# A GEGLU feed-forward kernel: x loaded in halves of the model dimension, first weights in 128 KB pieces over both queues

## The chip, the core and the metric

The kernel runs on one core of a Trainium2 chip. A core has a matrix engine (TensorE, "PE" in the profile; its weight loads are "PEld"), a vector engine (VectorE, "DVE"), a scalar engine (ScalarE, "ACT"), GpSimd ("POOL") and SyncE ("SP"). SBUF is the on-chip memory with 128 partitions, PSUM holds the matrix engine's sums in eight banks. Data come from device memory by DMA; here SP and ACT issue DMAs on a hardware queue each (q1 and q10 in the profile) and POOL issues them on a software queue (q0). An engine works through its program in order, and a DMA that it issues is one step of that program. The metric is the device time in microseconds (us).

## The reference

```python
B, S, D, F = 32, 32, 1024, 3584
x: (B, S, D), w_gate, w_up: (D, F), w_down: (F, D)      # bf16
def reference(x, w_gate, w_up, w_down):
    return (gelu(x @ w_gate) * (x @ w_up)) @ w_down     # gelu by the tanh formula
```

So there are N = 1024 tokens, a model dimension of 1024 and a hidden dimension of 3584.

## The kernel before

The kernel has two stages, and each engine has a program written out by hand (`prog_sp`, `prog_act`, `prog_pool`, `prog_pe`, `prog_dve`); semaphores tie them together.

Stage 1 computes hT, the hidden activations with the hidden dimension on partitions, in 28 chunks of 128 hidden units. A chunk needs a gate product G and an up product U. Each is a sum over eight slices of the model dimension (dk 0 to 7) of a 128x128 piece of weights times xT, the transposed x. Row 8p+dk of the weights stands on partition p in slice dk, so that a partition reads one contiguous row for each slice. ACT applies the GELU to G (L383, result in one of four buffers `tb`), DVE multiplies it by U out of PSUM and writes hT (L409). Stage 2 computes out = hT.T @ w_down in 17 jobs of 28 matmuls (L367), which ACT and DVE evict and SP stores.

The work of stage 1 is cut into "parts". Parts 0 to 7 are chunks 0 to 7 for tokens 0 to 255, one PSUM bank each (G in one half of the bank, U in the other). Parts 8 to 15 are the same chunks and banks for tokens 256 to 511, so part 8 can't start before part 0's product has left bank 0, and so on. From part 16 on a part has 512 tokens and two banks. The list `steps` sets PE's order: `together(range(0, 8), 6)` runs slices 0 to 5 over all eight parts side by side (8 G matmuls, 8 U matmuls for each slice), then slices 6 and 7 part after part; `together(range(8, 12), 5)` does the same with four parts and five slices; all others run one after the other.

x comes in three pieces of tokens, XA (0 to 255), XB (256 to 511) and XC2 (512 to 1023). It is put untransposed into `xs`, a part of hT that is written late, and DVE transposes it into xT in 32x32 blocks, one instruction for each piece and slice (L402): T0 to T7 of XA, then B0 to B7 of XB, then C0 to C7 of XC2. The order of DVE's work is written out in `dve_order`: the products E0 to E15 of parts 0 to 15 stand between the transposes.

The weights of chunks 0 to 7 (`wgbig` and `wubig`) are loaded by `early_loads`, which SP runs as side 0 and ACT as side 1. ACT runs it at the head of its program, before its first GELU. On each side there are 16 DMAs, in this order: two of XA (128 KB each, 512 bytes a packet), four of the weights of slices 0 and 1 (128 KB, 1 KB a packet), six of slices 2 to 7 (256 KB, 2 KB a packet; SP loads `wg`, ACT `wu`), two of XB (128 KB, 512 bytes a packet), two of XC2 (256 KB, 512 bytes a packet). The later chunks' weights come in DMAs of 1 MB by `load_w`, `wg` on SP and `wu` on POOL, once PE has finished with the buffer; the first of them wait for XC2 (`gate_w`).

Before its first real matmul PE runs NDUMMY = 9 matmuls of 512 columns on constants (L324), and waits for the last of them.

Of the kernel before, what the change touches and what calls it, by code (L numbers as in the profile page):

```python
# [5 lines left out]
P = 128  # L6
# [78 lines left out]
def bass_standalone__geglu_ffn__sampling_kernel(  # L85
# [7 lines left out]
    xf = x.flatten_outer_dims()  # L93
# [5 lines left out]
    DK = D // P  # L99
# [21 lines left out]

    XC = N // 32
    XE = D // 4
    XA, XB, XC2 = (0, 256), (256, 512), (512, 1024)
    XPIECES = [XA, XB, XC2]
    W0 = [(0, 0, 512), (0, 512, 1024), (1, 0, 512), (1, 512, 1024)]
    W0 += [(k, 0, 1024) for k in range(2, DK)]

    parts = []
    for t0, t1 in (XA, XB):
        for m in range(NBIG):
            parts.append((m, t0, t1, (m, 0, 256), (m, 256, 512)))
    NSHORT = len(parts)
# [4 lines left out]
    NPART = len(parts)  # L142
# [10 lines left out]

    steps = []

    def together(ps_, ks):
        for dk in range(ks):
            for key in ("G", "U"):
                for p in ps_:
                    steps.append((p, key, dk))  # L160
        for p in ps_:
            for key in ("G", "U"):
                for dk in range(ks, DK):
                    steps.append((p, key, dk))

    together(range(0, 8), 6)
    together(range(8, 12), 5)
    for p in range(12, NPART):
        together([p], 0)


    dve_order = [("T", dk) + XA for dk in range(DK)]
    mix = "E0 E1 B0 E2 B1 E3 B2 E4 B3 E5 B4 E6 B5 E7 B6 B7 C0 E8 C1 E9 C2 E10 E11 C3 C4 E12 C5 E13 C6 E14 C7 E15"
    for w in mix.split():
        if w[0] == "E":
            dve_order.append(("E", int(w[1:])))
        else:
            dve_order.append(("T", int(w[1:])) + (XB if w[0] == "B" else XC2))
    dve_order += [("E", p) for p in range(NSHORT, NPART)]

    jobs = []
# [9 lines left out]
        return ji % 2 == 0  # L191

    out_r = of.rearrange("(tc p) d -> p tc d", p=P)
    x_r = xf.rearrange("(c i) (a e) -> a i c e", i=32, a=4)
    wg_r = w_gate.rearrange("(p k) f -> p k f", k=DK)
    wu_r = w_up.rearrange("(p k) f -> p k f", k=DK)
    wd_r = w_down.rearrange("(m p) d -> p m d", p=P)

    C_PE = _Clock("pe")
    C_ACT = _Clock("act")  # L200
    C_DVE = _Clock("dve")
    C_POOL = _Clock("pool")
    Q_X = {(q, s): _Clock(f"x{i}{s}", 16) for i, q in enumerate(XPIECES) for s in range(2)}
    Q_W0 = {(w, p): _Clock(f"{w}0k{p[0]}c{p[1]}", 16) for p in W0 for w in ("wg", "wu")}
    Q_WG = [_Clock(f"wg{j}", 16) for j in range(NG)]
    Q_WU = [_Clock(f"wu{j}", 16) for j in range(NG)]
    Q_WD_SP = _Clock("wd_sp", 16)
# [5 lines left out]
    ctx = _Ctx()  # L213

    with ExitStack() as es:
# [24 lines left out]
        def wbuf(w, buf):  # L240
            if buf == "s":
                return small[w]
            o = 0 if buf == "lo" else GSZ * P
            return big[w][:, :, o:o + GSZ * P]
# [9 lines left out]
        def load_w(ew, eng, w, j):  # L254
            c0, gsz, buf = groups[j]
            q = (Q_WG if w == "wg" else Q_WU)[j]
            ctx.set((w, j), ew.do(lambda: eng.dma_start(  # L257
                wbuf(w, buf)[:, :, 0:gsz * P], w_r[w][:, :, c0 * P:(c0 + gsz) * P]), clock=q))

        def load_x(ew, eng, q, side):  # L260
            c0, c1 = q[0] // 32, q[1] // 32
            for a in (2 * side, 2 * side + 1):
                v = ew.do(lambda: eng.dma_start(
                    xs[32 * a:32 * (a + 1), c0:c1, :], x_r[a, :, c0:c1, :]), clock=Q_X[(q, side)])
            ctx.set(("x", q, side), v)

        def load_w0(ew, eng, w, p):
            k, f0, f1 = p
            ctx.set((w + "0", p), ew.do(lambda: eng.dma_start(
                big[w][:, k, f0:f1], w_r[w][:, k, f0:f1]), clock=Q_W0[(w, p)]))  # L270

        def early_loads(ew, eng, side):
            load_x(ew, eng, XA, side)
            for k in range(2):
                for w in ("wg", "wu"):
                    load_w0(ew, eng, w, W0[2 * k + side])
            for k in range(2, DK):
                load_w0(ew, eng, ("wg", "wu")[side], W0[2 + k])
            load_x(ew, eng, XB, side)
            load_x(ew, eng, XC2, side)  # L280

        def gate_w(ew, j):
            if war[j] is None:
                for s in range(2):
                    ew.wait(Q_X[(XC2, s)], ctx.get(("x", XC2, s)))
                return -1
            ew.wait(C_PE, ctx.get(("U", last_part[war[j]])))
            return war[j]
# [26 lines left out]
                    osb[:, tc, col0:col0 + ncols]), clock=Q_OUT)  # L315
            sp.wait(Q_OUT, last)

        NDUMMY = 9

        def prog_pe(eng):  # L320
            pe = _Eng(ctx, eng, C_PE)
            v = None
            for i in range(NDUMMY):
                v = pe.do(lambda: eng.matmul(ps[:, 7, :], ones_w, ones_x,  # L324
                                             start=True, stop=True), mark=(i == NDUMMY - 1))
            pe.wait(C_PE, v)
            opened = set()
            for (i, key, dk) in steps:
                m, t0, t1, gs, us = parts[i]
                w, (bank, f0, f1) = ("wg", gs) if key == "G" else ("wu", us)  # L330
                buf, slot, j = slot_of[m]
                if j is None:
                    p = next(p for p in W0 if p[0] == dk and p[1] <= m * P < p[2])
                    pe.wait(Q_W0[(w, p)], ctx.get((w + "0", p)))
                else:
                    pe.wait((Q_WG if w == "wg" else Q_WU)[j], ctx.get((w, j)))
                if bank in bank_before[i]:
                    pe.wait(C_DVE, ctx.get(("D", bank_before[i][bank])))
                for q in XPIECES:
                    if q[0] < t1 and t0 < q[1]:  # L340
                        pe.wait(C_DVE, ctx.get(("T", dk, q)))
                first = (i, bank) not in opened
                opened.add((i, bank))
                last = (dk == DK - 1)
                v = pe.do(lambda: eng.matmul(  # L345
                    ps[:, bank, f0:f1],
                    wbuf(w, buf)[:, dk, slot * P:(slot + 1) * P],
                    xT[:, dk, t0:t1],
                    start=first, stop=last and (key == "U" or gs[0] != us[0]),
                ), mark=last)  # L350
                if last:
                    ctx.set((key, i), v)
            pe.wait(Q_WD_SP, ctx.get("wd_sp_total"))
            pe.wait(Q_WD_POOL, ctx.get("wd_pool_total"))
            bank_last_job = {}
            for ji, (tc, col0, ncols, b) in enumerate(jobs):
                if b in bank_last_job:
                    pj = bank_last_job[b]
                    pe.wait(C_ACT if evac_eng_is_act(pj) else C_DVE, ctx.get(("E", pj)))
                else:  # L360
                    pe.wait(C_DVE, ctx.get(("D", owner[b])))
                bank_last_job[b] = ji
                v = None
                for m in range(FM):
                    pe.wait(C_DVE, ctx.get(("D", last_part[m])))
                    last = (m == FM - 1)
                    v = pe.do(lambda: eng.matmul(  # L367
                        ps[:, b, 0:ncols],
                        hT[:, m, tc * P:(tc + 1) * P],
                        wd[:, m, col0:col0 + ncols],  # L370
                        start=(m == 0), stop=(m == FM - 1),
                    ), mark=last)
                ctx.set(("O", ji), v)
# [18 lines left out]
        def prog_dve(eng):  # L392
            dve = _Eng(ctx, eng, C_DVE)

            for what in dve_order:
                if what[0] == "T":
                    dk, q = what[1], what[2:]
                    for s in range(2):
                        dve.wait(Q_X[(q, s)], ctx.get(("x", q, s)))
                    src = xs[:, q[0] // 32:q[1] // 32, :].rearrange(  # L400
                        "p c (j k) -> p c j k", k=DK)[:, :, :, dk]
                    ctx.set(("T", dk, q), dve.do(lambda: eng.transpose(  # L402
                        xT[:, dk, q[0]:q[1]].rearrange("p (c i) -> p c i", i=32), src)))
                else:
                    i = what[1]
                    m, t0, t1, _gs, (ub, u0, u1) = parts[i]
                    dve.wait(C_ACT, ctx.get(("A", i)))
                    dve.wait(C_PE, ctx.get(("U", i)))
                    ctx.set(("D", i), dve.do(lambda: eng.tensor_tensor(  # L409
                        hT[:, m, t0:t1], t_bufs[i % NTB][:, 0:t1 - t0], ps[:, ub, u0:u1], ALU.mult)))  # L410
# [56 lines left out]
```

## Time and profile before

| what | number |
|---|---|
| median of 3 runs | 301.82 us (301.38 to 302.17) |
| the profiled execution | 300.94 us, of which the span from first to last instruction is 299.6 us |
| first real matmul of PE | 5.60 us |
| idle of PE between 5.60 and 35.1 us | at 16.5, 19.7, 20.5 and 25.5 us, the longest 0.6 us |
| first GELU of ACT | 16.86 us |
| DVE waits for a DMA of x | until 4.83 us, and 1.06 us until 19.19 us |
| start of part 16 on PE | 35.12 us |
| start of stage 2 on PE | 200.83 us |

The span begins with the first instruction of the program; the 1.3 us between span and device time lie outside the instructions. In a timeline row stand the start, the length, the engine, the line, the operation, what it writes and reads, and the number of merged instructions; "SPq" and "ACTq" are the engine's sequencer, here issuing a DMA. In a row of the windows, busy time and number of instructions of each engine are followed by the granted TensorE clock, the mean busy share of the 16 DMA engines and what they moved in GB/s.

### The profile page before, as it was taken

How to read it: one execution, taken by the hardware profiler on the slowest of the kernel's cores; microseconds unless marked ns; L12 is line 12 of the kernel's file. 1: busy time of each engine (PE TensorE's matmuls, PEld its weight loads, DVE VectorE, ACT ScalarE, POOL GpSimd, SP SyncE). 2: the span in 40 equal slices, each digit the busy share in tenths (PEclk: the TensorE clock that was granted, in tenths of full speed). 3: DMA queues.
4: the chain of work that ended last, by engine and by line, in shares of the span. 5: the costliest groups of instructions: out<-in, count | busy, mean ns of one | idle time of the engine just before them, and what ended most of it. 6: DMA issues, size and time to landing. Idle time of an engine off the chain costs nothing.

```text
span 299.6 us, 3392 instructions
## 1 busy us (share of the span) xinstructions
PE 294.0 (98%) x1485; PEld 147.6 (49%) x1509; DVE 60.2 (20%) x96; ACT 41.4 (14%) x75; POOL 7.0 (2%) x12
## 2 busy tenths in 40 slices
PE   7999999999999999999999999999999999999997
PEld 3878744444444444444444444444444444444456
DVE  3259811211111211111211112210000000000000
ACT  1042211111211111211111211110000000000000
POOL 0001001020001002000000000000000000000000
DMA  8998002947007400952103000000000100010001
GB/s 239 381 223 270 13 1 81 343 142 278 2 0 251 171 0 7 357 198 63 77 0 142 0 0 2 0 0 18 20 18 18 35 20 18 18 36 19 18 18 37
DMA packets 19118, 26.43 MB, mean 88 GB/s; under 512 B 1056, under 2 KB 13472, under 8 KB 19104
## 3 DMA queue, kind: packets, MB, share of 16 engines
q1 hardware_dynamic: 13344, 14.68, 15.0%
q0 software_dynamic: 2176, 8.39, 7.9%
q10 hardware_dynamic: 3584, 3.15, 3.4%
q8 instruction: 12, 0.20, 0.3%
q14 instruction: 2, 0.02, 0.0%
HBM read 24.12 MB, written 2.10 MB: 87 GB/s over the span
## 4 chain that ended last, share of the span: by engine, by line
PE 97%; DMA 1%; issue 1%; DVE 1%; ACT 0%; DVEq 0%
PE ps L345 64%; PE ps L367 32%; DMA hT<-in_x_dram 1%; DVE xT L402 0%; ACT L377 0%; DVE hT L409 0%; ACT xT L389 0%; DVEq L41 0%
## 5 line engine op out<-in xcount | busy, mean ns | idle before, releaser
L367 PE MATMUL ps<-wd,hT 128*128 128x512 bf16 (+1 forms) x468 | 96.5, 366 | 0.4
L345 PE MATMUL ps<-xT,wgbig 128*128 128x512 bf16 (+1 forms) x378 | 78.6, 343 | 1.8 <-DVE xT L402 0.8
L345 PE MATMUL ps<-xT,wubig 128*128 128x512 bf16 (+1 forms) x379 | 78.8, 343 | 0.3
L367 PEld LDWEIGHTS ps<-wd,hT 128*128 128x128 bf16 x476 | 46.6, 98 | 50.4
L409 DVE TENSOR_TENSOR hT<-tb,ps 128x512 bf16<-128x512 f32 (+1 forms) x64 | 39.1, 613 | 140.8 <-PE ps L345 140.6
L383 ACT ACTIVATE tb<-ps 128x512 f32<-128x512 f32 (+1 forms) x64 | 34.8, 544 | 162.7 <-PE ps L345 161.2
L345 PEld LDWEIGHTS ps<-xT,wgbig 128*128 128x128 bf16 x384 | 37.4, 98 | 34.6 <-PE ps L324 1.7
L345 PEld LDWEIGHTS ps<-xT,wubig 128*128 128x128 bf16 x384 | 37.6, 98 | 31.9 <-DMA wubig<-in_w_up_dram 0.3
L345 PE MATMUL ps<-xT,wgsmall 128*128 128x512 bf16 x126 | 30.1, 379 | 0.1
L345 PE MATMUL ps<-xT,wusmall 128*128 128x512 bf16 x125 | 29.8, 379 | 0.2
L415 DVE CAST xT<-ps 128x512 bf16<-128x512 f32 (+1 forms) x8 | 5.3, 658 | 88.1 <-PE ps L367 88.1
L345 PEld LDWEIGHTS ps<-xT,wusmall 128*128 128x128 bf16 x128 | 12.5, 98 | 15.1
L345 PEld LDWEIGHTS ps<-xT,wgsmall 128*128 128x128 bf16 x128 | 12.5, 98 | 15.1
L402 DVE STREAM_TRANSPOSE xT<-hT 128x256 bf16<-128x256 bf16 (+1 forms) x24 | 17.8, 771 | 5.9 <-DMA hT<-in_x_dram 5.9
L389 ACT ACTIVATE xT<-ps 128x512 bf16<-128x512 f32 (+1 forms) x9 | 5.2, 573 | 93.1 <-PE ps L367 93.1
L324 PE MATMUL ps<-const-bfloat16-1.0 128*128 128x512 bf16 x9 | 4.0, 629 | 0.8 <-PEq L452 0.8
L257 POOL DMA_DIRECT2D wubig<-in_w_up_dram x3 | 2.6, 883 | 64.8 <-PE ps L345 64.8
L257 POOL DMA_DIRECT2D wusmall<-in_w_up_dram x2 | 1.9, 960 | 48.5 <-PE ps L345 26.0
L251 POOL DMA_DIRECT2D wd<-in_w_down_dram x3 | 2.3, 762 | 19.1 <-PE ps L345 19.1
L324 PEld LDWEIGHTS ps<-const-bfloat16-1.0 128*128 128x128 bf16 x9 | 1.2, 141 | 2.7 <-issue 2.7
L377 ACT ACT_TABLE_LOAD x1 | 1.3, 1283 | 0.7 <-PEq L452 0.7
L377 ACT ACTIVATE warm<-const-float32-0.0 128x1 f32<-128x1 f32 x1 | 0.2, 202 | 0.0
(4 smaller groups left out, 0.4 us busy)
## 6 DMA issues: line engine op xcount, KB each, us to landing
wd<-in_w_down_dram SPq DMA_DIRECT2D x4, 1024.0 KB, 10.6
wgbig<-in_w_gate_dram SPq DMA_DIRECT2D x3, 1024.0 KB, 5.6
wubig<-in_w_up_dram POOLq DMA_DIRECT2D x3, 1024.0 KB, 9.5
wd<-in_w_down_dram POOLq DMA_DIRECT2D x3, 1024.0 KB, 10.1
wgsmall<-in_w_gate_dram SPq DMA_DIRECT2D x2, 1024.0 KB, 5.6
wusmall<-in_w_up_dram POOLq DMA_DIRECT2D x2, 1024.0 KB, 8.8
out_dram<-xT SPq DMA_DIRECT2D x15, 128.0 KB, 1.7
wgbig<-in_w_gate_dram SPq DMA_DIRECT2D x6, 256.0 KB, 7.6
```

What stands on the lines that cost most here:

```text
L251: ew.do(lambda: eng.dma_start(wd[:, a:b, :], wd_r[:, a:b, :]), clock=clock)
L257: ctx.set((w, j), ew.do(lambda: eng.dma_start(wbuf(w, buf)[:, :, 0:gsz * P], w_r[w][:, :, c0 * P:(c0 + gsz) * P]), clock=q))
L324: v = pe.do(lambda: eng.matmul(ps[:, 7, :], ones_w, ones_x, start=True, stop=True), mark=(i == NDUMMY - 1))
L345: v = pe.do(lambda: eng.matmul(ps[:, bank, f0:f1], wbuf(w, buf)[:, dk, slot * P:(slot + 1) * P], xT[:, dk, t0:t1], start=first, stop=last ...
L367: v = pe.do(lambda: eng.matmul(ps[:, b, 0:ncols], hT[:, m, tc * P:(tc + 1) * P], wd[:, m, col0:col0 + ncols], start=(m == 0), stop=(m == F ...
L377: act.do(lambda: eng.activation(warm[:, 0:1], const0, ACTF.Gelu_apprx_tanh))
L383: ctx.set(("A", i), act.do(lambda: eng.activation(t_bufs[i % NTB][:, 0:t1 - t0], ps[:, gb, g0:g1], ACTF.Gelu_apprx_tanh)))
L389: ctx.set(("E", ji), act.do(lambda: eng.activation(osb[:, tc, col0:col0 + ncols], ps[:, b, 0:ncols], ACTF.Copy)))
L402: ctx.set(("T", dk, q), dve.do(lambda: eng.transpose(xT[:, dk, q[0]:q[1]].rearrange("p (c i) -> p c i", i=32), src)))
L409: ctx.set(("D", i), dve.do(lambda: eng.tensor_tensor(hT[:, m, t0:t1], t_bufs[i % NTB][:, 0:t1 - t0], ps[:, ub, u0:u1], ALU.mult)))
L415: ctx.set(("E", ji), dve.do(lambda: eng.tensor_copy(osb[:, tc, col0:col0 + ncols], ps[:, b, 0:ncols])))
```

## The change

Row 4p+k of each half of the model dimension now stands on partition p, so slices 0 to 3 come from the first half of x's columns and slices 4 to 7 from the second. x is loaded in six pieces (three of tokens, each in two halves), in packets of 256 bytes; a piece is still four DMAs, two on each side. The first weights are loaded in the order in which PE uses them, `wu` on SP and `wg` on ACT (but for the very first piece of `wg`, whose halves go to both): 128 KB pieces with 1 KB packets for slices 0 to 4, one DMA of 256 KB with 2 KB packets for slice 5, and 256 KB with 1 KB packets for slices 6 and 7 together. The second half of XA stands behind the weights of slices 0 to 3. On SP 26 DMAs and on ACT 25 replace the 16.

PE takes slices 0 to 4 in groups of four parts (parts 0 to 3, then 4 to 7), slice 5 over all eight, and then for each group slice 6 side by side and slice 7 part after part. The order of DVE's work follows; B0 now stands behind E3. The 1 MB loads become two of 512 KB, one for each half. NDUMMY is 8.

```diff
+    XPIECES = [t + (hh,) for t in (T_A, T_B, T_C) for hh in range(2)]
+    EARLY = [("x", XPIECES[0]), ("w", "wg", (0, 1), (0, 256), 0), ("w", "wg", (0, 1), (256, 512), 1)]
+    pieces = [("wu", 0, 0), ("wg", 0, 1), ("wu", 0, 1)]
+    pieces += [(w, k, g) for k in (1, 2, 3) for g in (0, 1) for w in ("wg", "wu")]
+    for i, (w, k, g) in enumerate(pieces):
+        EARLY.append(("w", w, (k, k + 1), (512 * g, 512 * g + 512), i % 2))
+    EARLY += [("x", XPIECES[1])]
+    for k, f0, f1 in ((4, 0, 512), (4, 512, 1024), (5, 0, 1024)):
+        EARLY += [("w", "wg", (k, k + 1), (f0, f1), 1), ("w", "wu", (k, k + 1), (f0, f1), 0)]
+    for f0, f1 in ((0, 512), (512, 1024)):
+        EARLY += [("w", "wg", (6, 8), (f0, f1), 1), ("w", "wu", (6, 8), (f0, f1), 0)]
+    EARLY += [("x", q) for q in XPIECES[2:]]
...
-    together(range(0, 8), 6)
-    together(range(8, 12), 5)
+    first, second = range(0, 4), range(4, 8)
+    for dk in range(5):
+        run(first, [dk])
+        run(second, [dk])
+    run(range(0, 8), [5])
+    for ps_ in (first, second):
+        run(ps_, [6])
+        for p in ps_:
+            run([p], [7])
+    run(range(8, 12), range(0, 5))
...
-    mix = "E0 E1 B0 E2 B1 E3 B2 E4 B3 E5 B4 E6 B5 E7 B6 B7 C0 E8 C1 E9 C2 E10 E11 C3 C4 E12 C5 E13 C6 E14 C7 E15"
+    for w in ("A0 A1 A2 A3 A4 A5 A6 A7 E0 E1 E2 E3 B0 B1 E4 B2 E5 B3 E6 E7 B4 B5 B6 B7 "
+              "C0 E8 C1 E9 C2 E10 C3 E11 C4 E12 C5 E13 C6 E14 C7 E15").split():
...
-    x_r = xf.rearrange("(c i) (a e) -> a i c e", i=32, a=4)
-    wg_r = w_gate.rearrange("(p k) f -> p k f", k=DK)
+    x_r = xf.rearrange("(c i) (hh a e) -> hh a i c e", i=32, hh=2, a=4)
+    wg_r = w_gate.rearrange("(hh p k) f -> p hh k f", hh=2, k=KH)
...
+            for hh in range(2):
                 v = ew.do(lambda: eng.dma_start(
+                    wbuf(w, buf)[:, hh * KH:(hh + 1) * KH, 0:gsz * P],
+                    w_r[w][:, hh, :, c0 * P:(c0 + gsz) * P]), clock=q)
...
+            for it in EARLY:
+                if it[0] == "x":
+                    t0, t1, hh = q = it[1]
+                    for a in (2 * side, 2 * side + 1):
+                        v = ew.do(lambda: eng.dma_start(
+                            xs[32 * a:32 * (a + 1), t0 // 32:t1 // 32, hh * 128:(hh + 1) * 128],
+                            x_r[hh, a, :, t0 // 32:t1 // 32, :]), clock=Q_X[(q, side)])
+                elif side == it[4]:
+                    _, w, (k0, k1), (f0, f1), _ = it
+                    ctx.set(it, ew.do(lambda: eng.dma_start(
+                        big[w][:, k0:k1, f0:f1],
+                        w_r[w][:, k0 // KH, k0 % KH:k0 % KH + k1 - k0, f0:f1]), clock=Q_W0[it]))
...
-        NDUMMY = 9
+        NDUMMY = 8
...
+                    src = xs[:, t0 // 32:t1 // 32, o:o + 128].rearrange(
+                        "p c (j k) -> p c j k", k=KH)[:, :, :, dk % KH]
```

## The prediction, made before the changed kernel ran

> **What bounds the kernel now.** I read the busy shares first, then the chain of work that ended last, then the timelines of the two issuing queues, the windows of the first 35 us, and the packets.
>
> ```profile
> PE 294.0 (98%) x1485; PEld 147.6 (49%) x1509; DVE 60.2 (20%) x96; ACT 41.4 (14%) x75; POOL 7.0 (2%) x12
> ```
>
> PE is busy for 294.0 of 299.6 us, so a change of loads can move only the start and PE's waits. The chain shows where these lie:
>
> ```profile
> 1.22 3.50 DMA hT<-in_x_dram
> 4.83 0.64 DVE xT L402
> ...
> 5.60 14.08 PE ps L345 x126
> ...
> 20.05 0.63 DVE xT L402
> 20.68 0.31 DVE hT L409
> 21.04 4.43 PE ps L345 x39
> 25.51 9.56 PE ps L345 x86
> ...
> 35.12 10.74 PE ps L345 x49
> ```
>
> PE starts at 5.60 us, behind XA's landing and the first transpose. Parts 0 to 15 are 256 matmuls of 256 columns at 0.109 us (eight start within 0.87 us): 27.9 us. They take 35.12 - 5.60 = 29.5 us, so 1.6 us are waits: 0.3 us for weights at 16.5 us, the rest from 19.7 to 25.5 us for transposes of XB and for products leaving PSUM. After 35.12 us I see no wait that depends on the early loads. The stretch from 19 to 35 us has a second limit, DVE:
>
> ```profile
> 20.00:25.00 5.00, 4.44 (x40) 3.73 (x41) 5.00 (x13) 0.77 (x2) 1.03 (x1) 1.00 0.33 79
> 25.00:30.00 5.00, 4.96 (x47) 4.22 (x45) 4.86 (x9) 1.67 (x5) 0.00 (x0) 1.00 1.06 368
> 30.00:35.00 5.00, 5.00 (x47) 4.48 (x46) 5.00 (x8) 1.01 (x3) 0.00 (x0) 1.00 0.05 15
> ```
>
> DVE is full there, with E0 to E15 and the transposes of XB and XC2. Whatever delays E0 delays this whole row of work. E0 begins on ACT, and ACT issues DMAs first:
>
> ```profile
> 6.61 5.89 ACTq L263 DMA_DIRECT2D hT<-in_x_dram  x4
> 16.86 0.38 ACT L383 ACTIVATE tb<-ps 128x256 f32<-128x256 f32 x1 [14.63 <-PE ps L345]
> ...
> L263 SPq DMA_DIRECT2D hT<-in_x_dram x6: 383/442/4060, 0.7 to 7.9; - x6
> L263 ACTq DMA_DIRECT2D hT<-in_x_dram x6: 390/475/4405, 0.8 to 8.1; - x6
> ```
>
> The last two rows give the shortest, median and longest issue of x on each queue. An issue takes 0.44 to 0.48 us, but the sixteenth and last took 4.06 us on SP and 4.41 us on ACT. They stood still from 7.92 to 11.98 and from 8.10 to 12.51 us. The landings say until when: the ninth DMA of the two queues landed at 11.74 and 12.39 us, the tenth at 13.12 and 13.75. Counted in packets for one of the 16 DMA engines (a DMA's packets divided by 16, and one more for its semaphore), the queue held six weight loads of 9, two of XB of 17 and one of XC2 of 33, or 121; the sixteenth adds 33, which makes 154. It went through when three weight loads were gone: 127. The fifteenth went through at 121 to 130. So I read a queue that holds about 128 packets per engine and makes the issuing engine wait beyond that. A limit in DMAs doesn't fit (nine were outstanding at both issues), one in bytes neither: the fifteenth passed at 2,048 KB or more with itself, while the sixteenth, at 1,792 KB with itself after the second of the three landings, still waited. Before, ACT had 4.3 us to spare until 16.86 us.
>
> **The change, part by part.** Packet rates come from windows in which one size moved:
>
> ```profile
> 5.00:6.75 1.75, 1.15 (x11) 1.07 (x12) 1.75 (x4) 0.00 (x0) 0.00 (x0) 1.00 1.09 353
> 7.00:9.50 2.50, 2.50 (x25) 2.24 (x24) 2.09 (x5) 0.00 (x0) 0.00 (x0) 1.00 1.06 385
> 12.00:14.50 2.50, 2.50 (x25) 2.23 (x24) 0.00 (x0) 0.00 (x0) 0.00 (x0) 1.00 1.05 402
> 15.50:20.25 4.75, 4.65 (x42) 3.64 (x40) 1.90 (x5) 2.32 (x7) 0.00 (x0) 1.00 1.20 288
> ```
>
> On each of 16 engines, 353 GB/s in 1 KB packets is 46.4 ns a packet, 385 to 402 in 2 KB 83 ns, 288 in 512 bytes 28.4 ns. From 2 KB to 1 KB a packet falls by 36.6 ns, from 1 KB to 512 bytes by 18. No row has 256 bytes. The lower end continues the line, 19.4 ns; the upper end is the price of 512 bytes, 28.4. As the three rows lie on one line I take 21 ns, near the lower end.
>
> *The queue.* ACT now issues 25 DMAs: per engine 34 packets for XA's first half, 9 + 63 for weights, 34 for XA's second half, 61 for weights, 34 + 34 for XB, 66 + 66 for XC2. Ahead of the last one (33) stand 33 + 66 of XC2, together 132, over 128. So it can't be issued before the DMA engines have worked off all weights, XA and XB. SP's list ends alike. The DMA engines need from 1.76 us (the first data of before): 216 packets of 1 KB (10.02 us), 16 of 2 KB (1.33), 16 of 512 bytes (0.45), and 256 of 256 bytes at 21 ns (5.38; 4.97 to 7.27). That makes 18.94 us. The same sum for before, up to the ninth DMA of both queues (64 packets of 512 bytes, 64 of 1 KB, 48 of 2 KB), gives 10.53 us, and the blocked issues ended at 11.98 and 12.51: a lag of 1.45 to 2.0 us. With ACT's 2.0 its first GELU runs at 20.9 us (20.0 to 22.8), or 0.7 us later if room comes only with a whole DMA of 33.
>
> *What is late next.* Behind ACT's issue are queued all GELUs; for them wait E0 to E7 on DVE, B0 behind E3 in DVE's order, and PE's part 8, which needs bank 0 and B0. Four GELUs at 0.43 us (six take 2.57 from 16.86 on), the product E3 and a transpose of 0.64 us put B0's end 2.85 us behind the first GELU. From there DVE's order goes 0.64 for a transpose and 0.43 for a product; PE waits for it at slices 3, 4, 6 and 7, 1.57 us in all, and parts 8 to 15 need 13.97 us. So part 16 starts 18.4 us behind the first GELU. Before it was 35.12 - 16.86 = 18.26. The shift is therefore 20.9 + 18.4 - 35.12 = **+4.2 us** (+3.3 to +6.1, +6.8 with the whole DMA).
>
> *The earlier start.* XA's first half is 64 packets per engine at 21 ns instead of 28.4: it lands 0.5 us earlier (0 to 0.6), and the dummy left out takes 0.44 us (4.00 / 9) from the dummies' end at 4.78. PE starts at about 5.1 us. This buys nothing at the end: the pieces of slices 0 to 3 keep up (128 KB at 353 GB/s is 0.37 us, PE uses one in 0.437), but slice 4 waits for XA's second half and the last weights, whose packets end at 1.76 + 11.8 + 128 x 0.021 = 16.25 us and land some 1.1 us later; 12 matmuls (1.3 us) follow. PE is done with parts 0 to 7 at 18.7 us and then stands until 23.8 us. Without the stall behind ACT, the gain would be 0.5 us less the 0.65 us by which E0 comes later (106 matmuls ahead of it, before 100).
>
> *The clock.* A dummy of 512 columns takes 0.44 us, a real one later 0.216: the first 4 us run at half rate. After 5 us of idling PE may fall back to it; the longest idle here is 0.82 us, so no row tells. Between nothing and another 4 us at half rate (2 us lost), part of which lies under the 1.57 us of waits for DVE, I take +0.2 us. An eighth instead of a ninth dummy risks at most 0.25 us (0.5 us at half rate), covered by the same wait. [...]
>
> *Small packets.* The row of 512 bytes gives 288 GB/s against 385 to 402 in 2 KB. [...]
>
> *Transposes.* They read with a stride of 8 bytes instead of 16. The bound is between the 0.64 us of now and the 0.38 us of a product of the same 256 columns, -1.8 us on B0 and PE's waits behind it. I take nothing.
>
> *The rest.* The loads in two halves add an issue of about 0.5 us on SP (5 times; wd loads stand behind) and 0.9 on POOL. The first pair also waits for XC2's later end, some 5 us after the 22.4 us of now. `wusmall` landed at 31.0 us and is first used after eight parts of 3.45 us from 35.12, at 62.7: over 20 us of cover; the later pairs have 20 us and more. Without cover each would cost its 0.5 to 0.9 us.
>
> **The sum.** 300.94 us of the profiled execution + 4.2 + 0.2 = 305.3. The median lies 0.9 above the profiled execution, so I put 301.82 + 4.4 = **306.2 us**.
>
> **The rivals.** *No block.* The issue at 8.1 us stood still for a reason that doesn't return. Then ACT is free by 0.8 + 25 x 0.475 = 12.7 us, and E0 waits for slice 6's weights: packets end at 16.25 less 32 x 0.0464 = 14.8 us, + 1.1 to land, + 6 matmuls and PSUM (0.85): 16.75 us, or 17.7 at 28.4 ns, against 16.86. That is -0.1 to +0.8, **302.2 us**. For it speaks that only two issues show the block, against it that both end at the same count.
>
> *Faster: the early start is kept.* This needs ACT free before 16 us and 256-byte packets at 19.4 ns or less. E0 comes at 17.28 - 0.6 + 0.65 on DVE, the 1.06 us that DVE waited for XB at 18.1 us is gone, and DVE's full row ends 1.0 us earlier: **300.8 us**. For it speaks that DVE's wait for XB and PE's start are on the chain; against it, that more packets lie ahead of XB than before. It decides once XB lands before 17.7 us and ACT's last issue ends before 16.
>
> *Not what it says.* Even with slow packets x's first half could land no earlier than XA before (4.72 us), as 64 packets per engine are as many as before. That is the upper end of 28.4 ns above, 308 us.
>
> **How the numbers follow.** The block has 0.70, no block 0.14, faster 0.16. The block's own range: +3.3 with 1.8 off for quicker transposes, to +6.8 and 0.8 of the clock: 303.3 to 309.4. I give 301.9 to 309.0, which takes in the upper half of "no block" and leaves out "faster" and the far end. About 0.3% (0.9 us) is what a measurement of this kernel can tell from no change. Faster has 0.16; "no block" gives 0.10 within and, where landing takes the longer lag, 0.04 slower; slower has 0.74 in all.
>
> **What would show it.** In the changed kernel's timeline, issues of x on ACT and SP that last over 1 us, ACT's last issue ending near 20.4 us with the first GELU right behind, PE idle from about 19 to 24 us, part 16 near 39.5. The 256-byte packets at 19 to 28 ns show the rate. I am wrong if ACT has issued everything by 13 us, or if PE passes from part 7 to part 8 without a wait.

## The result, and the profile after

| | median | runs | ratio to before |
|---|---|---|---|
| before | 301.75 us (301.01 to 302.35) | 8 | |
| changed | 302.54 us (301.56 to 303.03) | 8 | 1.0032, interval 1.0017 to 1.0047 |
| changed, measured again beside other runs | 302.06 us (301.54 to 303.69) | 12 | 1.0013, interval 0.9998 to 1.0029 |

By the medians the change makes the kernel slower by 0.2 to 0.8 us, where 4.4 us was forecast. The first interval lies above 1, the second takes it in, so that a small loss is likely and its size is uncertain. The profiled execution of the changed kernel took 302.69 us, with a span of 301.4. That is 1.75 us over the profiled execution of before, which at 300.94 was one of the quicker ones: 0.8 us under its median, while this one is 0.15 over its own. So the two traces differ by about 1 us more than the first medians do.

From the page of the changed kernel, the busy shares, and from its answer on the tile that holds x and hT, the rows of DVE and the DMA issues (shortest, median and longest in ns):

```profile
PE 295.1 (98%) x1508; PEld 147.1 (49%) x1508; DVE 54.3 (18%) x96; ACT 40.7 (14%) x75; POOL 10.1 (3%) x17
```

```profile
L420 DVE STREAM_TRANSPOSE xT<-hT x24: 402/428/706, 3.7 to 35.8; 128x256 bf16<-128x256 bf16 x16, 128x512 bf16<-128x512 bf16 x8
L427 DVE TENSOR_TENSOR hT<-tb,ps x18: 381/412/687, 20.7 to 43.8; 128x256 bf16<-128x256 f32 x16, 128x512 bf16<-128x512 f32 x2
L287 SPq DMA_DIRECT2D hT<-in_x_dram x12: 382/744/2415, 0.7 to 19.2; - x12
L287 ACTq DMA_DIRECT2D hT<-in_x_dram x12: 396/713/2582, 0.8 to 19.2; - x12
```

The same row of transposes in the kernel before:

```profile
L402 DVE STREAM_TRANSPOSE xT<-hT x24: 590/628/1103, 4.8 to 34.8; 128x256 bf16<-128x256 bf16 x16, 128x512 bf16<-128x512 bf16 x8
```

DVE's busy time fell by 5.9 us, and the part of the transposes in it from 17.8 to 11.4 us: 0.43 instead of 0.63 us for 256 columns, 0.70 instead of 1.10 for 512. And the issues of x last up to 2.6 us, many of them, on both queues. ACT's timeline shows where they end (start, length, operation, count):

```profile
9.62 10.66 ACTq L287 DMA_DIRECT2D hT<-in_x_dram  x8
20.32 0.94 ACT L399 ACTIVATE tb<-ps 128x256 f32<-128x256 f32 x3 [18.10 <-PE ps L361]
```

Eight issues take 10.66 us, to 20.28, and the first GELU follows 0.04 us behind, at 20.32. The row puts its wait down to PE, but PE's last matmul of part 0 had started at 18.64 and ended at 18.9: the GELU was ready 1.4 us earlier and stood behind ACT's own issues. The chain of waits from there (start, length, what):

```profile
6.51 6.89 DMA hT<-in_x_dram
...
13.43 0.46 DVE xT L420
...
14.02 7.36 PE ps L361 x63
...
21.41 0.19 DVE hT L427
...
22.07 0.45 DVE xT L420
...
22.66 179.90 PE ps L361 x896
202.55 96.78 PE ps L383 x476
```

The chain runs through XA's second half, which lands at 13.41 us, and the weights of slice 4, then through the products, B0 and part 8 at 22.66 us. From there PE never waits again: in the kernel before it had 0.2 us of waits behind 25 us and reached stage 2 at 200.8, here it is there at 202.5. The loss lies ahead of part 8: it started at 19.98 us in the kernel before and is 2.7 us late here. Of this the changed kernel makes good 0.9 us behind it, as it doesn't have the waits of before at 20.3 and 25.3 us. PE's waits of more than 0.1 us, from the starts of its matmuls:

| PE waits at | before | changed | for |
|---|---|---|---|
| first real matmul | 5.60 | 4.34 | XA, or its first half |
| 4.7 us | | 0.92 | `wu` of slice 0, landed at 5.67 |
| 8.2 us | | 0.31 | `wu` of slice 2, landed at 8.61 |
| 12.5 us | | 1.43 | XA's second half, landed at 13.41, and `wg` of slice 4 at 13.80 |
| 15.7 to 19.3 us | 0.14 | 0.28 | weights; the last landed at 19.77 (before 16.50) |
| 19.6 to 21.2 us | 0.99 | 1.34 | E0 to E3 and B0 |
| 25.2 us | 0.20 | | transposes of XB |
| part 16 starts | 34.90 | 36.63 | |

The trace of before lacks the record of part 16's first matmul, so 35.12 us is its second; its U group starts at 36.63, eight matmuls of 0.216 us later than 34.90. PE starts 1.26 us earlier in the changed kernel and loses more than that on the way. How well the DMA engines deliver, by windows (the last two numbers of a row are the DMA engines' busy share and GB/s):

```profile
4.50:9.00 4.50, 3.59 (x32) 2.73 (x31) 0.65 (x2) 0.00 (x0) 0.00 (x0) 1.00 1.02 331
10.00:12.50 2.50, 2.50 (x26) 2.22 (x23) 0.00 (x0) 0.00 (x0) 0.00 (x0) 1.00 1.21 239
...
17.50:24.00 6.50, 5.32 (x48) 4.31 (x47) 3.26 (x10) 2.32 (x8) 0.00 (x0) 1.00 1.34 217
```

In the first row 1 KB weights move, in the second weights and XA's second half, in the third weights and then x alone. The engines are busy in all three and move a third less once 256-byte packets are among them. For the third row the straight line of the prediction is enough: 5,241 packets of 256 bytes at 19.4 ns and 51 of 1 KB at 46.4 make 6.5 us on 16 engines. In the second, 652 and 407 of them make 2.0 us, and 2.5 went by.

### The profile page after: what moved, and what is told of

It is laid out like the page before. It is cut to its first block, busy times and chain, and to the rows that moved or that the text cites. A ratio compares the mean times of both kernels' runs of the same rounds, so it can differ in the third digit from the quotient of the medians.

```text
span 301.4 us, 3445 instructions
## 1 busy us (share of the span) xinstructions
PE 295.1 (98%) x1508; PEld 147.1 (49%) x1508; DVE 54.3 (18%) x96; ACT 40.7 (14%) x75; POOL 10.1 (3%) x17
## 4 chain that ended last, share of the span: by engine, by line
PE 94%; DMA 2%; SPq 2%; issue 0%; DVE 0%; ACT 0%; DVEq 0%
PE ps L361 62%; PE ps L383 32%; DMA hT<-in_x_dram 2%; SPq L293 1%; SPq L287 0%; DVE xT L420 0%; ACT xT L405 0%; DVE hT L427 0%; DVEq L41 0%
## 5 line engine op out<-in xcount | busy, mean ns | idle before, releaser
L361 PE MATMUL ps<-xT,wgbig 128*128 128x512 bf16 (+1 forms) x384 | 79.7, 344 | 2.5 <-DVE xT L420 2.4
L361 PE MATMUL ps<-xT,wubig 128*128 128x512 bf16 (+1 forms) x384 | 79.6, 344 | 0.9 <-DMA wubig<-in_w_up_dram 0.8
L399 ACT ACTIVATE tb<-ps 128x512 f32<-128x512 f32 (+1 forms) x64 | 34.0, 546 | 165.2 <-PE ps L361 165.2
L361 PEld LDWEIGHTS ps<-xT,wgbig 128*128 128x128 bf16 x384 | 37.1, 98 | 35.8 <-DMA wgbig<-in_w_gate_dram 2.0
L361 PEld LDWEIGHTS ps<-xT,wgsmall 128*128 128x128 bf16 x128 | 12.5, 98 | 15.1
L361 PEld LDWEIGHTS ps<-xT,wusmall 128*128 128x128 bf16 x128 | 12.5, 98 | 15.1
L420 DVE STREAM_TRANSPOSE xT<-hT 128x256 bf16<-128x256 bf16 (+1 forms) x24 | 11.4, 509 | 12.0 <-DMA hT<-in_x_dram 12.0
L277 POOL DMA_DIRECT2D wubig<-in_w_up_dram x6 | 4.5, 749 | 61.4 <-PE ps L361 61.4
L277 POOL DMA_DIRECT2D wusmall<-in_w_up_dram x4 | 3.1, 783 | 51.2 <-DMA hT<-in_x_dram 25.9
L270 POOL DMA_DIRECT2D wd<-in_w_down_dram x3 | 2.3, 765 | 18.5 <-PE ps L361 18.5
```

What stands on the lines that cost most here:

```text
L270: ew.do(lambda: eng.dma_start(wd[:, a:b, :], wd_r[:, a:b, :]), clock=clock)
L277: v = ew.do(lambda: eng.dma_start(wbuf(w, buf)[:, hh * KH:(hh + 1) * KH, 0:gsz * P], w_r[w][:, hh, :, c0 * P:(c0 + gsz) * P]), clock=q)
L361: v = pe.do(lambda: eng.matmul(ps[:, bank, f0:f1], wbuf(w, buf)[:, dk, slot * P:(slot + 1) * P], xT[:, dk, t0:t1], start=first, stop=last ...
L399: ctx.set(("A", i), act.do(lambda: eng.activation(t_bufs[i % NTB][:, 0:t1 - t0], ps[:, gb, g0:g1], ACTF.Gelu_apprx_tanh)))
L420: ctx.set(("T", dk, (t0, t1)), dve.do(lambda: eng.transpose(xT[:, dk, t0:t1].rearrange("p (c i) -> p c i", i=32), src)))
```

## The experiments

All were made from the kernel before or the changed one by the edits shown. Times are medians, with the ratio to the kernel before that ran beside them. The medians of kernels that did not run beside each other are best compared by these ratios.

**All late x on SP.** XB and XC2 leave ACT's queue.

```diff
+                    late = t0 >= 256
+                    if late and side == 1:
+                        ctx.set(("x", q, side), 0)
+                        continue
-                    for a in (2 * side, 2 * side + 1):
+                    for a in (range(4) if late else (2 * side, 2 * side + 1)):
```

> The changed kernel, with XB and XC2 issued by SP alone; ACT has no x behind the weights. Theory A (the weights' and x's DMAs are slow, and the full queue on ACT adds to it): ACT has issued everything by 13 us, the first GELU moves from 20.3 to about 18.9 us (part 0 is ready on PE at 18.7), part 8 starts at 21.4 to 21.9 instead of 22.66 because XB's first half lands at 20.8, and the time falls by 0.8 to 1.3 us, to 301.2 to 301.8. Theory B (the full queue alone makes the loss): part 8 starts before 20.5 us, the time falls by 2 us or more, below 300.6. Theory C (the queue is no part of it, DMA supply alone): part 8 still at 22.5 or later, time within 0.4 us of the changed kernel's 302.5.

Measured 301.53 us, ratio 0.9992 (0.9979 to 1.0006): the loss is gone. ACT had issued everything by 9.5 us, the first GELU ran at 19.07, part 8 at 21.40, as theory A had it. But the last weights also landed earlier, at 18.5 us instead of 19.77, so the run doesn't tell the full queue from the mixing of packets. It shows a third thing, in PE's timeline:

```profile
5.93 1.06 PE L365 MATMUL ps<-xT,wubig 128*128 128x256 bf16 x4
6.78 1.06 PE L365 MATMUL ps<-xT,wgbig 128*128 128x256 bf16 x4
...
9.91 0.60 PE L365 MATMUL ps<-xT,wgbig 128*128 128x256 bf16 x4
10.35 0.60 PE L365 MATMUL ps<-xT,wubig 128*128 128x256 bf16 x4
```

Four matmuls of 256 columns start within 0.85 us until 9.5 us and within 0.44 afterwards: the first 4 us of real work ran at half rate in this execution.

**Quick transposes in the kernel before.**

```diff
-                    src = xs[:, q[0] // 32:q[1] // 32, :].rearrange(
-                        "p c (j k) -> p c j k", k=DK)[:, :, :, dk]
+                    o = (dk // 4) * 128
+                    src = xs[:, q[0] // 32:q[1] // 32, o:o + 128].rearrange(
+                        "p c (j k) -> p c j k", k=4)[:, :, :, dk % 4]
```

> The kernel before, with the transposes reading at a stride of 8 bytes instead of 16 (the columns of x that a slice gets are others than the weights' rows, so the output isn't the reference's; all work is done). Theory A (the stride makes the transposes quick): they take 0.35 to 0.45 us for 256 columns and 0.70 for 512 instead of 0.63 and 1.09, DVE is no longer full from 20 to 35 us, PE's waits at 20.5 and 25.5 us go, PE starts 0.1 to 0.2 us earlier, and the time falls by 0.5 to 1.3 us, to 300.5 to 301.3. Theory B (the transposes are quick in the changed kernel for another reason, such as the smaller packets' landing or fewer collisions): 0.63 and 1.09 us as before, time within 0.3 us of 301.75.

```profile
L403 DVE STREAM_TRANSPOSE xT<-hT x24: 401/427/705, 5.3 to 34.3; 128x256 bf16<-128x256 bf16 x16, 128x512 bf16<-128x512 bf16 x8
```

Theory A: with nothing but the stride changed, a transpose takes what it takes in the changed kernel. The time is 301.13 us, ratio 0.9984 (0.9969 to 0.9999). PE's wait at 25 us is gone, those around 20 us are 1.0 us as before. The quick transposes are worth 0.5 us (0.0 to 0.9 by the interval) to a kernel whose loads come in time.

**XB and XC2 in 512-byte packets.**

```diff
-    XPIECES = [t + (hh,) for t in (T_A, T_B, T_C) for hh in range(2)]
+    XPIECES = [T_A + (0,), T_A + (1,), T_B + (2,), T_C + (2,)]
...
+                            xs[32 * a:32 * (a + 1), t0 // 32:t1 // 32, :],
+                            x_r2[a, :, t0 // 32:t1 // 32, :]), clock=Q_X[(q, side)])
```

> The changed kernel, with XB and XC2 loaded as before in whole pieces of 512-byte packets (two DMAs a side each; their columns are permuted against the weights' rows, so the output isn't the reference's). XA stays in halves. Theory A: the packets halve in number, XB lands by 20.3 us instead of 20.8 and 22.0, ACT's last issue ends by 18.5 us, the first GELU at about 18.9; part 8 is then bound by the weights and starts at 21.3 to 21.9 us; time 301.2 to 301.8. Theory B (the weights' late landing comes from the 256-byte packets of XB behind them): the last weights land before 18.5 us instead of 19.77, and the time falls below 300.8. Theory C (neither matters): 302.2 to 302.8.

Measured 302.05 us, ratio 1.0019 (1.0000 to 1.0038). The trace did what theory A said: ACT's last issue ended at 14.6 us, the first GELU ran at 18.44, part 8 started at 21.3, the last weights landed at 18.9. The median did not; it is where the changed kernel was when measured again, and one of the twelve runs took 304.89. Inconclusive.

**Slow transposes in the changed kernel.**

```diff
+                    if t0 > 0:
+                        src = xs[:, t0 // 32:t1 // 32, :].rearrange(
+                            "p c (j k) -> p c j k", k=DK)[:, :, :, dk]
```

> The changed kernel, with the transposes of XB and XC2 reading at a stride of 16 bytes as before (each waits for both halves of its piece; the columns that they take are others than the weights' rows, so the output isn't the reference's). Theory A (the step of my sum that failed is the transposes' price): they take 0.63 and 1.09 us, B0 ends 0.2 us later, PE waits for transposes at slices 3 to 7 of parts 8 to 11, part 16 starts at 38.0 to 38.7 us instead of 36.6, and the time rises by 1.4 to 2.0 us, to 303.9 to 304.5. Theory B (DVE had room anyway, as it waits for products from ACT): under 0.5 us more.

```profile
L424 DVE STREAM_TRANSPOSE xT<-hT x24: 401/610/1101, 3.9 to 39.1; 128x256 bf16<-128x256 bf16 x16, 128x512 bf16<-128x512 bf16 x8
```

Measured 303.44 us, ratio 1.0072 (1.0046 to 1.0099): by the ratios 1.2 us over the changed kernel as first measured and 1.8 over the second time, from seven runs. With the slow transposes the change would have cost 1.4 to 3.0 us by the interval. They took 0.63 and 1.10 us, but the rest of theory A missed: 303.44 lies under its range, and in the traced execution, which took 305.39, PE waited for transposes ahead of part 8 alone. Behind that it ran at half rate from 24.9 to 28.3 us and didn't wait for DVE again; part 16 started at 39.26. Two of the seven executions have a mean granted clock of 0.994, this one and the one at 304.78; the median of the other five is 302.88. So the slow transposes cost time, but part of the 1.2 to 1.8 us is the clock.

**A standing ACT by itself.** With x on SP, ACT waits for XB's landing before its first GELU.

```diff
             early_loads(act, eng, 1)
+            act.wait(Q_X[(XPIECES[3], 0)], 64)
```

> The kernel with XB and XC2 issued by SP alone, and ACT made to wait for the landing of XB's second half (about 21.3 us) before its first GELU: a standing ACT by itself, with the DMAs as they were. Theory A (a late first GELU moves all that follows): the first GELU at about 21.3 us instead of 19.07, part 8 at 23.8 to 24.2 instead of 21.4, time 2.2 to 2.8 us over the 301.5 without the wait, 303.7 to 304.4. Theory B (the late GELU is hidden by the weights and XB, and it was the queueing of x among the weights that cost the changed kernel its time): less than 0.6 us more.

Measured 305.51 us, ratio 1.0112 (1.0075 to 1.0149). The first GELU ran at 22.36 instead of 19.07, 3.3 us later, as XB's second half landed at 22.34 in this trace and not at 21.3; the median rose by 4.0 us, where the expectation had up to 2.8. The clock has a part in this. The traced execution took 306.47:

```profile
24.70 0.60 PE L365 MATMUL ps<-xT,wgbig 128*128 128x256 bf16 x4 [3.07 <-DVE xT L425]
25.13 0.60 PE L365 MATMUL ps<-xT,wubig 128*128 128x256 bf16 x4
25.57 0.81 PE L365 MATMUL ps<-xT,wgbig 128*128 128x256 bf16 x4
26.18 1.06 PE L365 MATMUL ps<-xT,wubig 128*128 128x256 bf16 x4
...
28.74 0.84 PE L365 MATMUL ps<-xT,wgbig 128*128 128x256 bf16 x4
29.42 0.60 PE L365 MATMUL ps<-xT,wubig 128*128 128x256 bf16 x4
```

The window from 26 to 27 us, with the granted clock in the third place from the end:

```profile
26.00:27.00 1.00, 1.00 (x6) 0.70 (x5) 1.00 (x4) 0.00 (x0) 0.00 (x0) 0.50 0.45 64
```

A microsecond after an idle time of 3.1 us PE fell to half rate, from 25.8 to 29.2 us, and the granted clock in the windows reads 0.50 there. Half of 3.4 us is lost by that. The mean clock tells which executions it hit: three at 0.994 took 305.3 to 306.5 us, one at 0.989 took 307.7, and the two at 1.0 took 303.74 and 303.77, 2.2 us over the kernel without the wait. So the standing ACT alone cost about 2.2 us, as theory A had it, and the clock the rest.

**Eleven dummies in the changed kernel** (`NDUMMY = 11`).

> The changed kernel with 11 dummies instead of 8, so that they last until about 5.5 us. Theory A (the start doesn't decide, the weights and the full queue do): first real matmul at 5.6 us at full clock, the waits at 4.7 and 12.5 us shrink by as much as the start is later, the first GELU still at 20.3; time within 0.4 us of 302.5. Theory B (8 dummies leave the first real matmuls at half rate in some executions, as in the run with x on SP where 20 pairs came 0.21 us apart): the median falls by 0.5 us or more, to 302.0 or less.

Measured 301.82 us, ratio 1.0010 (0.9998 to 1.0022). By the number this was theory B; but the first GELU ran at 19.40 us, straight behind ACT's last issue, and the last weights landed at 18.8, both a microsecond earlier than in the first trace. So it might have been the DMAs. That is why the changed kernel was measured again, below.

**2 KB packets for slices 4 to 7**, with x on SP, with 8 and with 11 dummies.

```diff
-    for k, f0, f1 in ((4, 0, 512), (4, 512, 1024), (5, 0, 1024)):
...
+    for k in (4, 5, 6, 7):
+        EARLY += [("w", "wg", (k, k + 1), (0, 1024), 1), ("w", "wu", (k, k + 1), (0, 1024), 0)]
```

> XB and XC2 on SP alone, and the weights of slices 4 to 7 in 256 KB loads of one slice with 2 KB packets, as before. Theory A (DMA supply of the weights bounds parts 0 to 7): the last weights land by 18.0 us instead of 18.5, the time falls by 0.2 to 0.7 us against 301.5, to 300.8 to 301.3. Theory B (PE's slow start bounds them, with 256 columns in 0.21 us until 9.4 us): within 0.2 us of 301.5.

> As the run before it, with 11 dummies. Theory A (without the full queue, PE's start at half rate is what is left): full clock from the first real matmul at 5.6 us, part 8 at 20.2 to 20.9 us, bound by the landing of XB's first half at 19.6, time 300.2 to 300.8, under the kernel before. Theory B (the extra dummies only delay the start): equal to or above the run with 8 dummies.

Measured 301.75 us, ratio 0.9999 (0.9991 to 1.0008), and 301.84, ratio 1.0005 (0.9996 to 1.0014). Neither gained as theory A had it: the first is 0.05 us above the range of its theory B, the second agrees with its own. With larger weight packets XA's second half landed at 14.24 and 14.26 us instead of 13.09, and PE stood 2.05 us for it in the first. How the packets of the two queues shared the DMA engines, no run shows.

**The changed kernel again.**

> The changed kernel itself, beside the three that follow on the same chip. It tells whether the 0.7 us that 11 dummies seemed to bring came from the dummies. Theory A (the landing of the DMAs varies between chips and executions, and the dummies do nothing): 301.7 to 302.1, with the first GELU before 20 us. Theory B (the dummies help): 302.3 to 302.8, as measured at first.

Measured 302.06 us, ratio 1.0013 (0.9998 to 1.0029). Here, too, the first GELU waits for ACT's last issue:

```profile
15.83 3.45 ACTq L287 DMA_DIRECT2D hT<-in_x_dram  x2
19.33 2.32 ACT L399 ACTIVATE tb<-ps 128x256 f32<-128x256 f32 x8 [17.11 <-PE ps L361]
```

The last issue ends at 19.29 us, the DMAs having run a microsecond faster than in the first trace. Against this run the eleven dummies gain 0.24 us, and the intervals overlap; against the first they gain 0.7. To judge by these traces, most of that was the landing of the DMAs, which varies from execution to execution.

**Both halves of XA first**, in the changed kernel; then with x on SP and 10 dummies, with 2 KB packets for slices 4 to 7 and without.

```diff
-    EARLY = [("x", XPIECES[0]), ("w",
+    EARLY = [("x", XPIECES[0]), ("x", XPIECES[1]), ("w",
...
-    EARLY += [("x", XPIECES[1])]
```

> The changed kernel with both halves of XA ahead of the weights; all else as it is. Theory A (the second half, in 256-byte packets among weights of 1 KB on the other queue, lands late and holds PE at slice 4): PE starts 0.7 to 1.2 us later, the wait of 1.4 us at 12.5 us goes, the weights' last landing is no later than 19.8 us, and the time is 0.2 to 0.9 us less than the changed kernel's. Theory B (the early start by the first half pays): 0.5 us or more above the changed kernel.

> Both halves of XA first, then the weights in order (2 KB packets for slices 4 to 7), XB and XC2 on SP alone, 10 dummies. Theory A (early loads are bound by the DMA engines, and small packets beside large ones on the other queue are what is slow): no x among the weights, the last weights land at 16.8 to 17.6 us, the first GELU at 17.3 to 18.3, part 8 at 19.4 to 20.2, time 300.3 to 301.0, under the kernel before (301.7). Theory B (the loads are bound by the bytes alone, however mixed): last weights after 18 us, time 301.4 or more.

> As the run before it, but with the changed kernel's 1 KB packets for slices 4, 6 and 7. Theory A (1 KB packets cost 46 ns where 2 KB cost 84): last weights 0.6 to 1.0 us later than in the run before, time 0.2 to 0.8 us more than it. Theory B (packet size of the weights doesn't matter): within 0.2 us of it.

The first measured 302.52 us, ratio 1.0030 (1.0012 to 1.0048), against theory A. The wait at slice 4 did go and the last weights landed at 18.5 us, but the traced execution had its first matmul at 5.74, 1.4 us behind the dummies, and ran at half rate from 6.5 to 12.1 us. The second measured 301.47, ratio 0.9999 (0.9981 to 1.0017), as its theory B had it; the third 301.18, ratio 0.9991 (0.9974 to 1.0008), under the ranges of both its theories. The 2 KB packets brought the last weights in at 18.1 us instead of 19.1 and the first GELU to 18.5 instead of 18.8; the medians don't follow, and packet size stays undecided. Three of the twelve runs of the third kernel took 302.5 to 302.7 us with a granted clock of 0.994 in all three; the other nine lay between 300.85 and 301.6.

**XC2 alone on SP.** `late = t0 >= 512` in the first edit: XB and the weights keep their mixture.

> The changed kernel with XC2 alone issued by SP; XA, XB and the weights stay on both queues as they are. ACT's list then ends with XB and never fills the queue past 12 to 14 us, while the DMAs up to XB run in the same mix as in the changed kernel. Theory A (ACT's full queue costs it): first GELU as soon as part 0 is ready, 18.2 to 19.2 us, some 0.5 to 1.4 us earlier; part 8 bound by the last weights and XB's first half, 21.0 to 21.8 us; time 301.4 to 301.9. Theory B (what helped with all x on SP was that the weights no longer shared the engines with XB): within 0.3 us of the changed kernel, 302.0 to 302.6.

```profile
9.91 3.52 ACTq L291 DMA_DIRECT2D hT<-in_x_dram  x4
19.03 1.21 ACT L403 ACTIVATE tb<-ps 128x256 f32<-128x256 f32 x4 [16.80 <-PE ps L365]
```

Measured 301.42 us, ratio 0.9996 (0.9984 to 1.0009). ACT's issues end at 13.43 us, the first GELU waits for PE and nothing else, and PE passes to part 8 with a wait of 0.13 us. The last weights land at 19.44 us, as late as in the changed kernel (19.77 and 18.91 in its two traces), and XA's second half at 13.63. So theory A: it is the full queue that made the changed kernel slower than before, and not that the weights shared the engines with XB. By the ratios the move of XC2 gains 0.5 to 1.1 us. The trace shows the place; the size is less sure, as the interval lies apart from that of the changed kernel as first measured, but overlaps with that of the second time.

**The clock, with x on SP:** 11 dummies with the changed kernel's order, and 13 with both halves of XA first.

> XB and XC2 on SP alone and 11 dummies. Theory A (after the full queue the half clock of the first real matmuls is what is left): first matmul at 5.5 to 5.7 us at full clock, part 8 at 20.2 to 21.0 us; time 300.7 to 301.2, and a narrower spread than the 300.6 to 302.35 with 8 dummies. Theory B (the clock isn't settled by the dummies, and the weights' landing bounds parts 0 to 7): 301.3 to 301.8, the same spread.

> XA first, XB and XC2 on SP, the changed kernel's weight pieces, 13 dummies instead of 10, which end at about 6.4 us, half a microsecond behind the first weights' landing. Theory A (the runs at 302.5 and more with 10 dummies are those where the clock fell back in the waits of 1 us before and behind the first matmuls): those runs go, median 300.8 to 301.2, none above 302. Theory B (they have another cause): two or three in twelve stay above 302.3, and the median is 0.2 to 0.5 us over 301.18.

The first measured 301.22 us (300.63 to 301.52), ratio 0.9987 (0.9974 to 1.0000), the second **300.83 us** (300.65 to 301.59), ratio 0.9978 (0.9966 to 0.9990). The first came out between the ranges of its two theories, the second in theory A's. Both spreads halve against the same kernels with 8 and 10 dummies (1.75 to 0.89 us, 1.85 to 0.94), no run lies above 301.6, and none has a mean clock under 1.0. This second kernel is the only one with the reference's output whose interval lies wholly under 1. Its PE, by the timeline and the chain:

```profile
0.78 5.42 PE L342 MATMUL ps<-const-bfloat16-1.0 128*128 128x512 bf16 x13 [0.78 <-PEq L473]
6.25 0.61 PE L364 MATMUL ps<-xT,wgbig 128*128 128x256 bf16 x4
```

```profile
7.24 193.57 PE ps L364 x1020
200.81 96.78 PE ps L386 x476
```

It starts real work 0.65 us later than the kernel before and waits only 0.54 us for `wu` of slice 0 and 0.13 at part 8. Its gain over the 10 dummies (0.35 us of the median) agrees with theory A on the clock. It was not run beside them on the same chip. Nor does its gain over the kernel before speak for the loads: the quick transposes alone gave 0.9984, and its stage 2 starts at 200.81 us, as in the trace of before (200.83).

## Why the prediction was right and wrong

*The full queue: right in place, and nearly in size.* ACT's last issue was to end just ahead of the first GELU, at 20.9 us (20.0 to 22.8). It did, at 20.3 and 19.3 in the two traces; the second is below the range. XC2 off ACT's queue takes the loss away, and a wait put there by hand moves the time. That about 128 packets per engine is the limit was inferred from two issues before, and is not confirmed. Counted from the packet records against what had been issued, ACT's stalled issue in the kernel before ended with 120 packets per engine still to go on average (its own included), and the last six in the changed kernel with 103 to 140.

*From the first GELU to part 16: the step that failed.* "Part 16 starts 18.4 us behind the first GELU" was the sum; it came 16.3 us behind (36.63 - 20.32), and 16.3 in the second trace too. Three quarters of the 2.1 us are one term: PE's 1.57 us of waits for DVE at slices 3 to 7. From 22.66 us to part 16 PE had no such wait. The term was wrong in two ways. The larger is the spacing of DVE's work. I took 0.64 us for a transpose and 0.43 for a product from their durations, but in the kernel before they start 0.56 and 0.30 us apart, since one begins before the record of the last one ends:

```profile
19.76 0.38 DVE L409 TENSOR_TENSOR hT<-tb,ps 128x256 bf16<-128x256 f32 x1
20.05 0.63 DVE L402 STREAM_TRANSPOSE xT<-hT 128x256 bf16<-128x256 bf16 x1
20.60 0.38 DVE L409 TENSOR_TENSOR hT<-tb,ps 128x256 bf16<-128x256 f32 x1
20.89 0.64 DVE L402 STREAM_TRANSPOSE xT<-hT 128x256 bf16<-128x256 bf16 x1
```

The smaller is the transposes' price, for which I had the bound of 0.38 in hand, wrote -1.8 us beside it and took nothing. My estimate of the shares: with DVE's starts from the run with slow transposes (0.55 and 0.30 us apart) and PE at its full rate, PE would wait 0.3 us, at slice 7. So some 1.2 us of the 1.57 were the spacing and 0.3 the stride; no run has the two apart at full rate.

The other 0.5 us lie ahead of part 8, which started 2.34 us behind the first GELU and not 2.85 (the terms named for it add up to 2.8). B0's own transpose gave 0.2. The GELUs and products gave the rest: waiting in a row, eight GELUs took 2.32 us, 0.28 each, where I had 0.43 from six that PE fed one by one. The run with the stride changed alone shows what made the transposes quick: in the kernel before they went from 0.63 to 0.43 us for 256 columns and from 1.10 to 0.70 for 512. Why a stride of 8 bytes is quicker than one of 16, it doesn't show.

*The pieces keep up: wrong, and hidden by the first.* I let PE finish parts 0 to 7 at 18.7 us and stand for 5 us. It finished at 21.3 and stood for 1.3. 128 KB at 353 GB/s was too good: 331 in the stretch of the weights, and 239 beside XA's second half, which I had among the weights at 21 ns a packet and nothing for the others. The last weights landed at 19.8 us (18.9 in the second trace) instead of 17.4; the two stretches account for 0.8 us of that, the rest is open. In the changed kernel this lay under the full queue. It is the whole of what the earlier start lost: PE began 1.26 us earlier and gave back 2.9 us of waits by 19.3 us.

*The clock after the stall: not in the changed kernel,* for PE stood 1.3 us and not 5. The 0.2 us taken fall away. In the traces where PE stood 2.0 us (slow transposes) and 3.1 us (standing ACT) it did fall to half rate.

*The sum.* First GELU 20.3 instead of 20.9, part 16 16.3 instead of 18.4 us behind it: 36.63 us, a shift of +1.7 against the true 34.90, where +4.4 was forecast. The medians say +0.2 to +0.8, in part since the trace of before was of a quick execution; the prediction had noted that and yet added the whole shift to the median. The 35.12 us also made the waits of before 1.6 us, where they are 1.4. "No block" forecast 302.2 us, close to the measured time, but its condition did not hold: the block is in both traces. "Faster" failed on the same block and on XB, whose first half landed at 20.8 us and not before 17.7. "Not what it says" failed too: x's first half landed at 3.62 us, XA before at 4.72. The loads in two halves cost nothing, as said: `wusmall` was there at 35.8 us, well before 62.7.

## What to carry to other kernels

An engine that issues DMAs ahead of its own computing must be able to issue them all: count the packets that stand in its queue, not the DMAs (here an issue of ACT passed in 0.47 us with ten DMAs of its queue outstanding, and the last took 1.05 us with eight, then six; counted in packets, the issues stood still with some 100 to 140 per engine), and give the late ones to an engine with nothing else to do. Before an earlier start is bought with smaller pieces, add up when the last piece that the stage needs will land; here the start came 1.26 us earlier and the last weights 3.3 us later. When work on an engine is added up, take the distance between starts and not the durations: here that made some 1.2 us of a miss of 2.1. And where a sum has a bound of -1.8 us that no row excludes, look for what decides it before taking nothing.

## What the runs showed of the hardware

- XA's second half, in packets of 256 bytes, landed at 12.9 to 13.6 us beside weights in packets of 1 KB in nine traces, and at 14.2 and 14.3 us beside 2 KB in two.
- By the packet records, a packet of 256 bytes took 17 to 18 ns while the first half of XA moved alone, under the 19.4 ns of the straight line. Where all of x moved from both queues, the records read 25 ns but overlap (busy share 1.34), and the number of packets moved fits 19.4 ns. So the trace shows no extra price of small packets by themselves, and of the prediction's two prices the lower one held. Beside weights of 1 KB, from 10 to 12.5 us, the same prices fall short by 0.5 us.
- PE's release from half rate is not settled by a number of dummies. In the changed kernel's trace it had come by the first real matmuls behind 8 dummies (four of 256 columns in 0.61 us); with 11 in an unbroken row the first four still started within 0.83 us, and half rate lasted until 6.7 us in the trace; with gaps of 0.77 and 1.39 us behind 8 dummies it came at 9.5 and 12.1 us. In the kernel before the granted clock reads 1.00 from 0 to 5 us, while a dummy took 0.44 us and 512 columns later 0.216, so that at the start only the distance between the matmuls tells.
- Half rate came back after idle times of 2.0 us (the slow transposes) and 3.1 us (the standing ACT), 1.3 and 1.1 us after work had begun again, and by the distance between the matmuls lasted 3.4 us both times (24.9 to 28.3 and 25.8 to 29.2 us).
